# The means of the input's rows taken off x in place of off the weights, in a linear-attention and MLP-mixer kernel on one core

## The chip, the cores and the metric

The kernel runs on one core of one Trainium2 chip. The metric is the device time of one execution in microseconds; less is better. Times given for a kernel are medians of several executions; a profile is one further execution.

## The reference

The input x has 2048 rows of 512 columns. Each row is normalized, and two branches work on the result; the output is x plus the product of the first branch and a silu of the second. Cut to what matters:

```python
xn = _layernorm(x, axis=-1)
s = _A_ref(xn, A_wqkv, A_wo)           # linear attention, 32 heads of 16
g = _silu(_B_ref(xn, B_w1, B_w2, B_w3, B_w4))   # mixer block
return x + s * g

# _A_ref: q, k, v = xn @ wqkv
pq, pk = phi(q), phi(k)                # phi(t) = (t + 1 if t > 0 else exp(t)) + 1e-6
kv = einsum(pk, v); z = sum of pk over the rows
o = (pq @ kv) / (pq . z + 1e-6);  s = o @ wo

# _B_ref: h = gelu(_layernorm(xn) @ w1); its four quarters of 128 columns are shifted
# by +1, -1, +2 and -2 rows, then @ w2, x1 = xn + that;
# g = x1 + gelu(_layernorm(x1) @ w3) @ w4
```

The mean of a row has to be taken off before a product with wk, wq or w1. A product of the row less its mean with W is the product of the row with W less the mean times the sums of W's columns. So there are three ways: take the mean off x, subtract the column means from W once ("centring" W: then a row's mean drops out), or subtract mean times column sums from the product.

## The kernel before, in words

The rows are worked on in tiles of 128; four tiles (512 rows) are a block, and there are four blocks, b = 0 to 3. Products run in a split form: each operand is a rounded high part and a low rest, and a product is three passes, high x high, low x high, high x low (`products`). Pairs of tiles are multiplied by a scheme of seven quarter products in place of eight (`seven`, and for keys and queries `pair_kq`), which needs sums of operands (`forms_x`, `forms_q`, `forms_m`) and adds of results.

The stages, in order: load WK, WQ and the transposed input xt (`load_u`, which rounds it into u, high and low); the plain rows x for the means and variances (`load_rows`, `scale_x`); keys (`key`, `feature_k`) and queries (`query`), and the products of keys with rows (`gram`, tiles g), for block 0 singly, for block 1 half singly and half in pairs, for blocks 2 and 3 in pairs; the first mixer product with W1 (`mix1`, tiles h), with shifted rows and a halo of two columns at each edge of a block (`split_halo`); the second (`mix2`, tiles pbm, pem); the attention's matrix M from the grams, WV and WO; and then, block by block, the up products (tiles a, pa, pb, pe) and down products (acc) of the MLP, with the attention (`turn_q`, then for block 0 `attend`, tiles s, and for the others `forms_q` and `attend_pair`, tiles pas, pbs, pes) between them, and `gate` at the end.

How the means are handled before: WQ and W1 are centred by `Weights.center`: the four chunks are added on VectorE (for W1 by a load and three adding transfers, tile w1t), a full-precision product with ones gives the column sums in every row (tiles wqm, w1m), and four VectorE instructions subtract them from the weights. WK isn't centred: `sum_k` gets its column sums by eight products of its rounded chunks with ones (tile ksum), ScalarE makes wneg, their negative, and `feature_k` adds mean times wneg to a key's product. In `pair_kq`, ScalarE makes two tiles from wneg (ci, ck) for each pair, and two VectorE instructions add them. For blocks 2 and 3, `forms_x` takes two of its sums by loads and adding transfers (`by_dma`).

What sets the order: the program does not run in the order of the text. Every operation is recorded in a plan with an estimated duration (`Plan.add`), product by product; `deadlines` gives each product a nominal time and works back to a due time for everything that feeds it; `nudged` moves single due times by a table (SOONER); `emit` then takes, engine by engine, the operation that can start first by the plan's estimates, the one due soonest among equals, and writes it out. So each engine has a fixed order of its own and waits in it. Buffers are slots, 89 of tag "p", 4 accumulators and 4 product banks. Loads and stores are issued by SyncE (SP), adding transfers by GpSimd (POOL, `Plan.gather`). All TensorE instructions are recorded at line 146, ScalarE's at 168, most of VectorE's at 191, 196 and 201, loads at 207, stores at 212 and adding transfers at 225.

Of the kernel before, what the change touches and what calls it, by code (L numbers as in the profile page):

```python
# [85 lines left out]
class Plan:  # L86
# [54 lines left out]
    def mm(self, out, lhs, rhs, start, stop, slow=False, more=False, behind=None):  # L141

        nc = self.nc
        busy = 2 * (.0025 + .00083 * rhs.n) if slow else .0053 + .000444 * rhs.n
        self.add("PE", busy, busy + .17, [lhs, rhs], [behind or out],
                 lambda: nc.tensor.matmul(out.get(), lhs.get(), rhs.get(), start=start, stop=stop,  # L146
                                          skip_group_check=more))
# [81 lines left out]
    GAP = .06  # L229
    PATIENCE = 5.0  # L230
# [38 lines left out]
    def emit(self, first, lead, reserve, window, ahead, table=()):  # L269
# [20 lines left out]
        while left:  # L290
# [5 lines left out]
            for e, cands in avail.items():  # L296
                picks = []
                low = INF
                for op in cands:
# [11 lines left out]
                    for t in fresh:  # L311
# [7 lines left out]
                        s = max(s, q[need - 1][0] + self.GAP)  # L319
# [57 lines left out]
            for o in op.post:  # L377
# [5 lines left out]
                else:  # L383
                    r = op.end + self.GAP
# [11 lines left out]
def linear_attn_gated_by_mixer(  # L396
# [36 lines left out]
    counts = {"w": 2, "p": 89, "h": 6, "sm": 12, "ab": 2, "acc": 4, "mm": 4}  # L433
# [61 lines left out]
    onesr, bmask, few = fixed("onesr", P, F32R), fixed("bmask", P), fixed("few", 4)  # L495
# [3 lines left out]
    rs1, rs2, ns1, nm1, nm2, au, mr1 = (fixed(n, NT) for n in ("rs1", "rs2", "ns1", "nm1", "nm2", "au", "mr1"))  # L499
    arow = memory("arow", S + 2 * EDGE, 1)  # L500
# [18 lines left out]
    for o in (0, EDGE + S):  # L519
        pl.store(arow[:, o:o + EDGE], zacc[:1, :EDGE])  # L520
# [23 lines left out]
    class Weights:  # L544
# [25 lines left out]
        def center(self, by_dma=False):  # L570

            t, r = piece(self.name + "t"), self.raw
            if by_dma:
                pl.load(t, self.src[:, 0])
                for c in range(1, NC):
                    pl.gather(t, self.src[:, c])
            else:
                pl.tt(t, r[0], r[1], ALU.add)
                pl.tt(t, t, r[2], ALU.add)
                pl.tt(t, t, r[3], ALU.add)  # L580
            ps = bank(self.name + "m")
# [29 lines left out]
    def scale_x(lo, n):  # L611
# [7 lines left out]
        if lo >= QT:  # L619
# [11 lines left out]
    def spread_a(b):  # L631

        ps = pl.new("mm", f"ab{b}", F32, 512)[:QT, :P]
        pl.transpose(ps, au[:, b * QT:(b + 1) * QT], ident.all)
        t = pl.new("p", f"ar{b}", F32, PIECE)[:QT, :P]
        pl.act(t, ps, AF.Copy)
        row = arow[:, EDGE + b * BT:EDGE + (b + 1) * BT]
        pl.store(row.via(lambda ap: ap.rearrange("o (j p) -> (o j) p", p=P)), t)
# [11 lines left out]
    def load_u(b, parts):  # L650
# [3 lines left out]
        for q in range(parts):  # L654
            o = q * n
            for c in range(NC):
# [3 lines left out]
                pl.load(src, xt[b, c][:, o:o + n])  # L660
                hi, lo = (t[:, 2 + o:2 + o + n] for t in UT[b][c])
                if b == c == q == 0:
                    pl.ts(hi, src, 1.0, None, ALU.mult)
                    split(lo, src, hi)
                else:
                    rounded(hi, lo, src)

# [84 lines left out]
    def feature_k(i, ps):  # L752

        t, r = piece(f"kt{i}"), piece(f"kr{i}")
        pl.stt(t, wneg.all, mean(mv1, i), ps, ALU.mult, ALU.add)
# [9 lines left out]
    def key(i):  # L765
        ps = bank(f"k{i}")
        project(ps, i, WK, range(NC))
        feature_k(i, ps)
# [14 lines left out]
    def query(i):  # L783
# [3 lines left out]
        pl.act(z, ps, AF.Identity, scale=col(rs1, i), bias=one)  # L787
# [54 lines left out]
    def pair_kq(i):  # L842
# [32 lines left out]
        pl.stt(zk, pb, rk, ck, ALU.mult, ALU.add)  # L875
# [427 lines left out]
    wneg = fixed("wneg", 512)  # L1303
# [11 lines left out]
    load_u(0, 2)  # L1315
# [12 lines left out]
    sum_k(ksum, 0)  # L1328
    for c in range(1, NC):
        for i in range(2):  # L1330
            project(ks[i], i, WK, [c])
        sum_k(ksum, c)
    pl.act(wneg.all, ksum, AF.Copy, scale=-1.0)
# [6 lines left out]
    WQ.center()  # L1340
    WQ.split()
    gram(0)
    query(0)
    query(1)
    load_u(1, 1)
    for i in range(QT, 2 * QT):
        load_rows(i)
    gram(1)
# [6 lines left out]
    forms_x(1, 1)  # L1355
    early_s, early_f = EARLY
# [7 lines left out]
    for b in range(1, NQ):  # L1364
# [23 lines left out]
    pl.load(hal.all, halo.rearrange("p q c -> p (q c)"))  # L1388
    for b in range(NQ):
        scale_u(b)  # L1390
        spread_a(b)
# [15 lines left out]
    pool(.4, [], bmask.all, lambda: g.memset(bmask.all.get(), 0.5))  # L1407
    for base, s in ((0, 1), (DH - 1, -1)):
        v = bmask.all.via(lambda ap: ap.rearrange("p (h d) -> p h d", d=DH))
# [23 lines left out]
    for gg in range(NC):  # L1433
# [4 lines left out]
        pl.tt(kvt.cols(*cs), ps, bmask.all, ALU.mult)  # L1438
# [25 lines left out]
    for b in range(NQ):  # L1464
# [5 lines left out]
        for n, fs in enumerate(groups):  # L1470
# [11 lines left out]
            if b == 0 and 0 < n <= QT:  # L1482
                turn_q(n - 1)
            if b == 0 and 1 < n <= QT + 1:
                attend(n - 2)
            if b == 0 and n == QT:
                forms_m()
            pairs = []
            if b > 0:
                for k in range(2):  # L1490
                    if n == (2, 3)[k]:
                        for j in range(2):
                            turn_q(b * QT + 2 * k + j)
                        forms_q(b * QT + 2 * k)
                    if n == (4, 5)[k]:
                        pairs.append(b * QT + 2 * k)
# [102 lines left out]
```

## Time and profile before

| | before |
|---|---|
| median of 3 runs | 517.4 us (516.55 to 517.57) |
| profiled execution, its own time | 516.63 us |
| its span, first to last instruction | 514.9 us |
| granted TensorE clock | 0.999 |
| VectorE, ScalarE, GpSimd busy | 78%, 68%, 21% of the span |
| DMA | 105.24 MB, 204 GB/s in the mean |

The page names engines as PE (TensorE matmul), PEld (its weight loads), DVE (VectorE), ACT (ScalarE), POOL (GpSimd) and SP (SyncE); SPq and POOLq are the queues in which they issue transfers. Tile names stand as out<-in, with buffer numbers left out. The chain that ended last is followed back from the last instruction, at each step to what released it. Products are pipelined: a product's duration runs from its start to a modelled end and overlaps the next one, so what it costs is the step from its start to the start of the next.

### The profile page before, as it was taken

What the parts mean: (1) busy time and instruction counts of PE and PEld (TensorE: products, weight loads), DVE (VectorE), ACT (ScalarE), POOL (GpSimd) and SP (SyncE); (2) the same over time, 40 slices, a digit from 0 to 9 for tenths busy, and PEclk for the clock granted to TensorE, in tenths of its full rate; (3) what the DMA queues carried; (4) which work ended last, traced back from release to release, by engine and by line L of the source; (5) the groups of instructions that cost most, each with busy time, mean ns of one, the idle gap of its engine ahead of it and who ended that gap; (6) DMA issues with size and microseconds to landing.
All of it is one profiled execution on the core that took longest, in us unless ns stands there. A gap on an engine that the chain in (4) does not pass through costs nothing.

```text
span 514.9 us, 9112 instructions
## 1 busy us (share of the span) xinstructions
PE 508.0 (99%) x2987; PEld 440.4 (86%) x2987; DVE 402.0 (78%) x848; ACT 350.5 (68%) x759; POOL 109.4 (21%) x196
## 2 busy tenths in 40 slices
PE   8999999999999999999999999999999999999996
PEld 5778778877788897999899988899898998899985
DVE  4999998759989758999898649788576857497645
ACT  6797998977696678999986655467462555554621
POOL 3477163561100221232100022000230000410000
PEclk9999999999999999999999999999999999999999
DMA  7948858698642999899767589846499562897804
GB/s 230 281 112 225 238 178 212 169 225 231 137 153 71 229 287 273 246 282 305 266 220 240 197 199 235 239 152 178 113 192 308 162 209 91 176 293 219 274 3 120
DMA packets 77698, 105.24 MB, mean 204 GB/s; under 512 B 8228, under 2 KB 34356, under 8 KB 77652
## 3 DMA queue, kind: packets, MB, share of 16 engines
q1 hardware_dynamic: 67780, 87.63, 52.7%
q0 software_dynamic: 9872, 17.04, 20.0%
q8 instruction: 23, 0.38, 0.3%
q14 instruction: 23, 0.19, 0.1%
HBM read 69.64 MB, written 30.81 MB: 195 GB/s over the span
## 4 chain that ended last, share of the span: by engine, by line
PE 87%; ACT 4%; DMA 4%; DVE 2%; issue 2%; SPq 1%; POOL 0%; POOLq 0%; ACTq 0%; DVEq 0%
PE acc L146 21%; PE pb L146 11%; PE h L146 9%; PE g L146 7%; PE pe L146 5%; PE pbm L146 5%; PE pbx L146 4%; PE pbs L146 3%; PE q L146 3%; PE pa L146 2%; PE pem L146 2%; PE s L146 2%; PE pex L146 2%; PE pes L146 2%; PE a L146 2%
## 5 line engine op out<-in xcount | busy, mean ns | idle before, releaser
L225 POOL DMA_DIRECT2D xo<-x1d x12 | 10.6, 1034 | 151.5 <-ACT xo L168 151.0
L225 POOL DMA_DIRECT2D o<-xnd x16 | 13.9, 892 | 67.4 <-DMA w4d<-w_10l 29.8
L225 POOL DMA_DIRECT2D th<-in_x x14 | 12.1, 887 | 72.3 <-DVE th L201 62.5
L168 ACT ACTIVATE gf<-gf 128x512 f32<-128x512 f32 (+1 forms) x40 | 20.8, 522 | 0.8
L168 ACT ACTIVATE th<-xo 128x512 f32<-128x512 f32 (+1 forms) x16 | 9.7, 615 | 14.9 <-DVE xo L191 11.4
L168 ACT ACTIVATE p<-pe 128x256 f32<-128x256 f32 x20 | 7.6, 382 | 15.9 <-PE pe L146 15.6
L191 DVE TENSOR_TENSOR gf<-pa,p 128x256 f32<-128x256 f32 x20 | 8.3, 417 | 10.7 <-PE pa L146 7.3
L225 POOL DMA_DIRECT2D zacc<-ke x10 | 9.1, 911 | 29.8 <-DVE ke L201 14.2
L191 DVE TENSOR_TENSOR gf<-pb,p 128x256 f32<-128x256 f32 x20 | 8.4, 421 | 8.6 <-ACT p L168 4.6
L168 ACT ACTIVATE p<-pb 128x256 f32<-128x256 f32 x20 | 7.6, 380 | 9.0 <-PE pb L146 8.6
L191 DVE TENSOR_TENSOR f_10l<-gf,f_10h 96x512 fp32r<-96x512 f32 x4 | 2.7, 686 | 14.1 <-PE pb L146 13.9
L168 ACT ACTIVATE u<-pb 128x256 f32<-128x256 f32 x20 | 7.6, 382 | 8.8 <-PE pb L146 8.8
L191 DVE TENSOR_TENSOR ht<-h,abc 128x512 f32<-128x512 f32 x16 | 10.9, 689 | 2.7 <-PE h L146 2.6
L168 ACT ACTIVATE y<-o,nm,rs 128x512 f32<-128x512 f32 x16 | 11.8, 806 | 1.2 <-POOL nm L196 1.2
L196 POOL TENSOR_SCALAR w<-mv 128x4 f32<-128x4 f32 (+2 forms) x10 | 3.3, 329 | 43.3 <-DVE mv L196 42.9
L201 DVE SCALAR_TENSOR_TENSOR th<-th,so 128x512 f32<-128x512 f32 (+1 forms) x17 | 11.1, 659 | 1.5 <-ACT th L168 0.3
L168 ACT ACTIVATE xo<-acc 128x512 f32<-128x512 f32 x12 | 7.2, 598 | 7.3 <-PE acc L146 6.9
L168 ACT ACTIVATE ht<-ht 128x512 f32<-128x512 f32 x16 | 9.6, 623 | 3.4 <-DVE ht L191 3.4
L191 DVE TENSOR_TENSOR so<-so,xo 128x512 f32<-128x512 f32 (+1 forms) x16 | 10.7, 671 | 1.5 <-DMA xo<-x1d 1.3
L168 ACT ACTIVATE sq<-o,sx 128x512 f32<-128x512 f32 x16 | 11.4, 713 | 0.2 <-DVE sx L196 0.2
L201 DVE SCALAR_TENSOR_TENSOR qz<-pq,zb 128x512 f32<-128x512 f32 x16 | 10.9, 683 | 0.5 <-DMA pq<-pqd 0.5
L201 DVE SCALAR_TENSOR_TENSOR pq<-pq,rd 128x512 f32<-128x512 f32 x16 | 10.9, 688 | 0.3
(1717 smaller groups left out, 2277.1 us busy)
## 6 DMA issues: line engine op xcount, KB each, us to landing
w_s<-in_w SPq DMA_DIRECT2D x28, 256.0 KB, 5.3
x<-in_x SPq DMA_DIRECT2D x16, 256.0 KB, 4.6
xnd<-x SPq DMA_DIRECT2D x16, 256.0 KB, 3.8
pqd<-qr SPq DMA_DIRECT2D x16, 256.0 KB, 2.3
o<-xnd POOLq DMA_DIRECT2D x16, 256.0 KB, 6.7
x1d<-o SPq DMA_DIRECT2D x16, 256.0 KB, 4.7
pq<-pqd SPq DMA_DIRECT2D x16, 256.0 KB, 4.8
out<-th SPq DMA_DIRECT2D x15, 256.0 KB, 3.4
```

Of the source, the lines that this page charges most:

```text
L146: lambda: nc.tensor.matmul(out.get(), lhs.get(), rhs.get(), start=start, stop=stop, skip_group_check=more))
L168: nc.scalar.activation(out.get(), src.get(), func, scale=get(scale), **kw)
L191: self.vec(eng, out, [a, b], lambda: self.e(eng).tensor_tensor(out.get(), a.get(), b.get(), op=op), True)
L196: lambda: self.e(eng).tensor_scalar(out.get(), a.get(), get(s1), get(s2), **kw), False,
L201: lambda: self.nc.vector.scalar_tensor_tensor(out.get(), a.get(), get(s), b.get(), op0=op0, op1=op1),
L225: lambda: self.nc.gpsimd.dma_start(out.get(), get(src), accum_op=ALU.add), mb=mb)
```

## The change

Six things change.

- `load_u` for blocks 1 to 3, and once more for block 0 ahead of `mix1`, loads xt and then adds to it, by an adding transfer of POOL, a row of minus the means (nrow) that lies in memory and is broadcast over the partitions. `spread` makes that row: from the means and variances of the block's four tiles it puts two sets of four columns side by side (an), transposes them by one product (ab), copies it (ar) and stores it in two rows, arow (as before) and nrow. It now stands ahead of `load_u` of its block, and `load_rows` ahead of it. The halo has its means added too (`load_halo`).
- For block 0, xt is first used uncentred for its keys and queries: keys have mean times the column sums taken off as before, queries now likewise (qneg, cq).
- WQ and W1 aren't centred any more; keys of blocks 1 to 3 and the pairs have no term of means (ci, ck and their adds go).
- WK's column sums come from adding the four chunks on VectorE and one full-precision product, in place of eight products.
- Block 0's attention goes through `forms_q` and `attend_pair` as that of the other blocks. `forms_x` makes all its sums on VectorE.
- The plan: products are estimated a little shorter, an operation of another engine is taken to reach TensorE 0.16 us after its end in place of 0.06 (PE_GAP), there are 90 slots in place of 89, and a new SOONER table. The order of all engines is new.

```diff
-        busy = 2 * (.0025 + .00083 * rhs.n) if slow else .0053 + .000444 * rhs.n
+        busy = 2 * (.0025 + .00083 * rhs.n) if slow else .005 + .000443 * rhs.n
...
+    PE_GAP = .16
...
-                        s = max(s, q[need - 1][0] + self.GAP)
+                        s = max(s, q[need - 1][0] + (self.GAP if e != "PE" else self.PE_GAP))
...
-                    r = op.end + self.GAP
+                    r = op.end + (self.GAP if o.eng != "PE" else self.PE_GAP)
...
-        def center(self, by_dma=False):
...
-            if by_dma:
-                pl.load(t, self.src[:, 0])
-                for c in range(1, NC):
-                    pl.gather(t, self.src[:, c])
...
-            for c in range(NC):
-                pl.stt(r[c], ps, -1.0 / D, r[c], ALU.mult, ALU.add)
+        def sums(self, ps):
+            t, r = piece(self.name + "t"), self.raw
+            for c in range(1, NC):
+                pl.tt(t, t if c > 1 else r[0], r[c], ALU.add)
             pl.mm(ps, ones.all, t, True, True, slow=True)
...
-    def scale_u(b):
+    def spread(b):
+
+        u, m = (an[:, (2 * b + k) * QT:(2 * b + k + 1) * QT] for k in range(2))
         p = small(f"pu{b}", QT).all
         pl.ts(p, var(mv1, b * QT, b * QT + QT), 1.0 + EPS, EPS * EPS, ALU.mult, ALU.add, eng="POOL")
-        power(au[:, b * QT:b * QT + QT], p, QT)
+        pl.ts(m, means(mv1, b * QT, b * QT + QT), -1.0, None, ALU.mult, eng="POOL")
+        power(u, p, QT)
+        ps = pl.new("mm", f"ab{b}", F32, 512)[:2 * QT, :P]
+        pl.transpose(ps, an[:, 2 * b * QT:2 * (b + 1) * QT], ident.all)
+        t = pl.new("p", f"ar{b}", F32, PIECE)[:2 * QT, :P]
+        pl.act(t, ps, AF.Copy)
+        for k, row in enumerate((arow, nrow)):
+            dst = row[:, EDGE + b * BT:EDGE + (b + 1) * BT]
+            pl.store(dst.via(lambda ap: ap.rearrange("o (j p) -> (o j) p", p=P)),
+                     t.via(lambda ap, k=k: ap[k * QT:(k + 1) * QT]))
...
                 pl.load(src, xt[b, c][:, o:o + n])
+                if centred:
+                    pl.gather(src, nrow[:, EDGE + b * BT + o:EDGE + b * BT + o + n].via(
+                        lambda ap: ap.to_broadcast([P, n])))
...
-    def sum_k(ps, c):
-
-        for n, p in enumerate(WK.chunk(c)):
-            pl.mm(ps, onesr.all, p, c == n == 0, c == NC - 1 and n == 1)
...
-        pl.act(z, ps, AF.Identity, scale=col(rs1, i), bias=one)
+        if i < QT:
+            cq = piece(f"cq{i}")
+            pl.act(cq, qneg, AF.Identity, scale=col(mr1, i), bias=one)
+            pl.stt(z, ps, col(rs1, i), cq, ALU.mult, ALU.add)
+        else:
+            pl.act(z, ps, AF.Identity, scale=col(rs1, i), bias=one)
...
-        ci, ck = piece(f"ci{i}"), piece(f"ck{i}")
-        for t, n in ((ci, i), (ck, k)):
-            pl.act(t, wneg.all, AF.Identity, scale=col(mr1, n), bias=one)
         go(pb, "a11", "b11")
-        pl.stt(p1, pb, ri, ci, ALU.mult, ALU.add)
+        copy(p1, pb, ri)
...
-            load_u(b + 1, 1)
             for j in range(QT):
                 load_rows(t0 + QT + j)
+            spread(b + 1)
+            load_u(b + 1, 1)
             scale_x(t0 + QT, QT)
-            forms_x(b + 1, by_dma=True)
+            forms_x(b + 1)
...
-            W1.center(by_dma=True)
...
+    load_u(0, 1)
+    load_halo()
...
-            if b == 0 and 0 < n <= QT:
-                turn_q(n - 1)
-            if b == 0 and 1 < n <= QT + 1:
-                attend(n - 2)
-            if b == 0 and n == QT:
+            pairs = []
+            if b == 0 and n == 3:
                 forms_m()
-            pairs = []
-            if b > 0:
-                for k in range(2):
...
+            for k in range(2):
+                if n == (2, 3)[k] if b == 0 else n == (2, 3)[k]:
+                    for j in range(2):
+                        turn_q(b * QT + 2 * k + j)
+                    forms_q(b * QT + 2 * k)
+                if n == (4, 5)[k] if b == 0 else n == (4, 5)[k]:
+                    pairs.append(b * QT + 2 * k)
```

More of the change, by code (lines that the diff above doesn't have):

```diff
@@ L519, in linear_attn_gated_by_mixer @@
     for o in (0, EDGE + S):
-        pl.store(arow[:, o:o + EDGE], zacc[:1, :EDGE])
+        for row in (arow, nrow):
+            pl.store(row[:, o:o + EDGE], zacc[:1, :EDGE])
     def mean(mv, i):
@@ L666, in load_u, with load_halo @@
                     rounded(hi, lo, src)
+    def load_halo():
+        hm = small("hm", NQ * W)
+        pl.load(hal.all, halo.rearrange("p q c -> p (q c)"))
+        for o, k in ((-2, 0), (BT, 2)):
+            dst = hm.cut([(0, NQ * W)], 2 * NQ, lambda ap, k=k: ap.rearrange("p (b w) -> p b w", w=W)[:, :, k:k + 2])
+            src = nrow.cut([(0, S + 2 * EDGE)], S, lambda ap, o=o: ap[:, EDGE + o:EDGE + o + S].rearrange(
+                "o (b n) -> o b n", n=BT)[:, :, :2].to_broadcast([P, NQ, 2]))
+            pl.fetch(dst, src)
+        v = hal.all.via(lambda ap: ap.rearrange("p (b c w) -> p b c w", c=NC, w=W))
+        m = hm.all.via(lambda ap: ap.rearrange("p (b w) -> p b w", w=W)[:, :, None, :].to_broadcast([P, NQ, NC, W]))
+        pl.tt(v, v, m, ALU.add, eng="POOL")
     def split_halo(b):
@@ L754, in feature_k @@
         t, r = piece(f"kt{i}"), piece(f"kr{i}")
-        pl.stt(t, wneg.all, mean(mv1, i), ps, ALU.mult, ALU.add)
+        pl.stt(t, wneg, mean(mv1, i), ps, ALU.mult, ALU.add)
         pl.act(r, t, AF.Relu, scale=col(rs1, i))
@@ L874, in pair_kq @@
         go(pb, "a22", "t4", False)
[L875 removed]
+        copy(zk, pb, rk)
         phi_q(k, qk)
@@ L1331, in linear_attn_gated_by_mixer @@
             project(ks[i], i, WK, [c])
-        sum_k(ksum, c)
-    pl.act(wneg.all, ksum, AF.Copy, scale=-1.0)
+    WK.sums(ksum)
+    pl.act(wneg, ksum, AF.Copy, scale=-1.0)
     for i in range(2):
@@ L1339, in linear_attn_gated_by_mixer @@
     WQ = Weights("wq", wqkv[0])
-    WQ.center()
     WQ.split()
+    qp, qneg = bank("qsum"), piece("qneg")
+    WQ.sums(qp)
+    pl.act(qneg, qp, AF.Copy, scale=-1.0)
     gram(0)
```

59 lines of the change are left out of this document (23 added, 36 removed), and 50 rows, old and new, of the table SOONER.

## The prediction

> **What bounds the kernel now.** I read the head of the page first, then the chain, then the waits of TensorE, then the first 30 us of its timeline.
>
> ```profile
> span 514.9 us, 9112 instructions
> PE 508.0 (99%) x2987; PEld 440.4 (86%) x2987; DVE 402.0 (78%) x848; ACT 350.5 (68%) x759; POOL 109.4 (21%) x196
> ...
> PE 87%; ACT 4%; DMA 4%; DVE 2%; issue 2%; SPq 1%; POOL 0%; POOLq 0%; ACTq 0%; DVEq 0%
> ```
>
> TensorE is busy for 508.0 of 514.9 us and holds 87% of the chain. The view of waits, for PE alone, says how little it waits for others (total, times, longest):
>
> ```profile
> PE warm L146 <- POOL ones L506: 1.0, 1, 1.0
> PE ksum L146 <- ACT wk_1h L168: 0.3, 1, 0.3
> PE pb L146 <- DVE gf L191: 0.3, 1, 0.3
> PE pbx L146 <- DVE p1x L201: 0.3, 1, 0.3
> PE k L146 <- ACT u_1h L168: 0.3, 1, 0.3
> ```
>
> That is 2.2 us in all. So the time is the sum of the products' issue steps: taking products away shortens it directly, and a new wait on PE lengthens it directly. The steps come from the chain (start, us, what) and, below it, the timeline of PE (start, duration):
>
> ```profile
> 150.66 11.13 PE h L146 x48
> 277.10 2.48 PE s L146 x21
> 508.00 2.38 PE accx L146 x20
> ```
>
> ```profile
> 13.26 0.39 PE L146 MATMUL ksum<-wk_3h,onesr 128*128 128x512 f32 x1
> 13.49 0.39 PE L146 MATMUL ksum<-wk_3l,onesr 128*128 128x512 f32 x1
> 19.32 1.02 PE L146 MATMUL wqm<-wqt,ones 128*128 128x512 f32 x2
> 20.19 0.97 PE L146 MATMUL g<-k0h,x0h 128*128 128x512 f32 x3
> 23.80 0.40 PE L146 MATMUL q<-wq_0h,u_0l 128*128 128x512 f32 x1
> 24.34 0.50 PE L146 MATMUL q<-wq_0h,u_0h 128*128 128x512 f32 x1
> ...
> 26.87 0.39 PE L146 MATMUL q<-wq_2h,u_2h 128*128 128x512 f32 x1
> 27.26 0.50 PE L146 MATMUL q<-wq_2l,u_2h 128*128 128x512 f32 x1
> ```
>
> A row's duration (0.39) is longer than its step, since products overlap. A step of 512 columns is 11.13/48 = 0.232 us, of 256 columns 2.48/21 = 0.118 us, and a full-fp32 product of 512 columns, which runs in two passes, holds PE from 19.32 to 20.19, 0.87 us. PE's last product ends at 508.00 + 2.38 = 510.4; what PE isn't busy besides its waits is the tail behind it, 4.5 us.
>
> **The change part by part.** The base is the profiled execution: 516.63 us, of which 514.9 is span. It lies 0.8 us under the median of the runs (517.4).
>
> *WK's sums.* Eight ksum products go (8 x 0.232 = 1.86) and one fp32 product comes (0.87): **-0.99**. The DVE adds that feed it (three of 512 columns) run beside PE. Bounds: three of the eight stand ahead of the two starting waits for wk_1h and u_1h; if the data come no earlier, their 0.70 only lengthens those waits and -0.29 is left. On the other side x0's load is moved from the sixth place of SP's queue to the tenth, so xt0_1 lands after 896 KB in place of 1,280 KB, and both waits (0.6) may go: -1.59. I keep the middle.
>
> *W1 no longer centred.*
>
> The views of the tiles w1m and wqm (durations in ns, least, median, most; first and last start):
>
> ```profile
> L146 PE MATMUL w1m<-w1t,ones x2: 590/590/591, 125.5 to 125.9; 128*128 128x512 f32 x2
> L201 DVE SCALAR_TENSOR_TENSOR wq_s<-wqm,wq_s x4: 681/683/685, 21.0 to 23.6; 128x512 f32<-128x512 f32 x4
> ```
>
> The same two passes as wqm: **-0.87**. With it go four DVE instructions, a load and three POOL gathers, none on the path.
>
> *WQ no longer centred.* The product stays (qsum for wqm). What goes is the chain from it through DVE's four wq_s instructions (from 21.0 to 23.6 + 0.68 in the row above) to the q products. q's step from 23.80 to 24.34 is 0.54 and that from 26.87 to 27.26 0.39, in place of 0.232 each: 0.3 and 0.16 of waiting. I take **-0.4**, bounds -0.7 and 0. Late next are four added DVE instructions that put the means back in q of block 0, behind PE.
>
> *Block 0's attention.* The order of instructions shows 96 products of 256 columns before and 84 after, 12 x 0.118 = **-1.42**. What it costs is DVE work: 16 instructions of 256 columns and two more of 512, net.
>
> Two of the page's groups (xcount | busy, mean ns), and three stretches (length, PE, PEld, DVE, ACT, POOL, clock, DMA, GB/s):
>
> ```profile
> L191 DVE TENSOR_TENSOR gf<-pa,p 128x256 f32<-128x256 f32 x20 | 8.3, 417 | 10.7 <-PE pa L146 7.3
> ...
> L191 DVE TENSOR_TENSOR ht<-h,abc 128x512 f32<-128x512 f32 x16 | 10.9, 689 | 2.7 <-PE h L146 2.6
> ```
>
> ```profile
> 240.00:260.00 20.00, 19.98 (x137) 17.97 (x136) 18.13 (x52) 19.57 (x50) 5.37 (x8) 1.00 0.75 236
> 260.00:280.00 20.00, 20.00 (x137) 18.26 (x137) 19.29 (x40) 14.59 (x32) 0.00 (x0) 1.00 0.84 270
> 280.00:300.00 20.00, 20.00 (x120) 17.66 (x119) 13.41 (x23) 11.96 (x25) 0.00 (x0) 1.00 0.56 186
> ```
>
> DVE is busy 50.8 of 60 us, so 9.2 are free; added are 16 x 0.417 + 2 x 0.689 = 8.1. ACT, 46.1 busy, has 13.9 free and gains 3. It just fits, and the new order spreads single acc products between those of the attention, which PE can do meanwhile: 0. If the cover isn't there, see below.
>
> *The means off x.* Block 1's xt now waits for the means of its rows: DVE's row statistics, two small POOL results, a transposition on PE (ab), an ACT copy, a store to memory, a load that adds them in (a POOL gather), and only then the rounding. PE is in order, so both the ab product and the first k product of block 1 can stand and hold all behind them. By the order of instructions 39 products lie between the two: 39 x 0.232 = 9.0 us of cover. Queued behind it: on ACT behind ar, exp of q and k; on SP behind the store (itself behind two x loads), stores of q and x that nobody needs soon; on POOL behind the four gathers, block 2's statistics, which have time. The links, from the timelines and the chain, then from the tile ab, then from the DMA issues (us to landing last):
>
> ```profile
> 36.01 2.46 DVE L593 BATCH_NORM_STATS2 st<-x 128x6 f32<-128x512 f32 x4
> 42.42 0.94 POOL L225 DMA_DIRECT2D zacc<-kr  x1
> 44.27 1.11 POOL L609 TENSOR_TENSOR au<-pu,nhalf 128x4 f32<-128x4 f32 x1
> 45.51 1.28 POOL L225 DMA_DIRECT2D xf<-in_xt  x1
> 34.61 0.62 ACT L168 ACTIVATE u_1h<-xt 128x512 fp32r<-128x512 f32 x1
> 43.76 1.61 PE k L146 x7
> ```
>
> ```profile
> L151 PE MATMUL ab<-ident,au x4: 270/270/272, 133.6 to 134.9; 128*4 128x128 f32 x4
> L168 ACT ACTIVATE ar<-ab x4: 249/250/266, 134.0 to 135.2; 4x128 f32<-4x128 f32 x4
> ```
>
> ```profile
> w4d<-w_0h SPq DMA_DIRECT2D x1, 256.0 KB, 2.2
> x1d<-o SPq DMA_DIRECT2D x16, 256.0 KB, 4.7
> w1t<-in_w POOLq DMA_DIRECT2D x3, 256.0 KB, 4.7
> o<-xnd POOLq DMA_DIRECT2D x16, 256.0 KB, 6.7
> abc<-arow SPq DMA_DIRECT2D x4, 258.0 KB, 4.6
> ```
>
> Product 0.27, copy 0.25, store 2.2 to 4.7, gather 4.7 to 6.7, rounding 0.62: 8.0 to 12.5 us against 9.0, so a wait of 0 to 3.5 at the k products. Above it, the statistics: ab stands 9.0 us ahead of the k of 43.76 (less the 1.4 saved by then), near 33.3. The statistics ran at 36.01, but in the new order some ten DVE instructions of 0.6 that stood ahead now follow, and xt's loads come behind the x rows: they run at 28 to 30, with 2.46, the aggregation and 1.11 + 0.5 on POOL to 32.5 to 34.5: 0 to 1.2 at ab. Together 0 to 4.7. The nearest rows (a gather from memory into SBUF, 4.7, and a broadcast row of the same kind on SP, 4.6, no slower than plain loads) speak for the low end: **+1.0**, half at each.
>
> The Trainium skill ("DMA: Bandwidth & Descriptors", Anatomy of one DMA — SWDGE (gpsimd) path) fits a gather's time as 2.0 us plus bytes/436e3, an estimate of 2.6 us here; by it the k wait would be nothing and the sum 0.5 lower. The rows above, 4.7 to 6.7, do not agree, and stand.
>
> Blocks 2 and 3 have the same chain under 65 and 57 products (15.1 and 13.2 us) against 12.5: 0. The reloaded xt of block 0 waits for nothing late. Queues: POOL issues 16 gathers more and 7 fewer, SP 7 issues more.
>
> ```profile
> q0 software_dynamic: 9872, 17.04, 20.0%
> ```
>
> 65 gathers take 20.0% of 514.9, 1.6 us of all engines each; nine more are 14 us, mostly between 30 and 125 us, where no PE wait on a DMA is on the list above: 0.
>
> *Tail and order.* The last 38 products are the same ones in the same order as in the row of accx: 0. The new order elsewhere may gain or lose within what PE waits now: 0, bounds -0.6 and +1.
>
> Sum: -0.99 - 0.87 - 0.4 - 1.42 + 1.0 = **-2.7**, 513.9 against the profiled execution. Half of its distance to the median added, **514.3 us**.
>
> **The rivals.** *The chain of the means is late (slower).* Place: ab and the k products of block 1. Beyond the 4.7 above, the four gathers follow each other; each chunk feeds nine products, 2.1 us, and a gather that shares the engines with x8 to x11 may land 0.6 later than the last one's products end, three times: 6.5 in place of 1.0, 514.3 + 5.5 = **519.8**. For it: order on PE leaves no other work ahead of it. Against: gathers of 1.6 us fit in 2.1. It turns the sign from a wait of about 5.
>
> *The change doesn't do what it says at the start.* The start is paced by loads, ksum stood in front of waits, and wkt's DVE adds are late for the one product: -0.29 in place of -0.99, and nothing from q: 1.1 less, **515.4**. For it: the two waits of 0.3; against: at 13.3 us the step of ksum is 0.23, so PE was full there.
>
> *DVE becomes the bound in block 0.* Of its 9.2 free us 6.6 lie in 280 to 300, behind part of the added 8.1; if 2.5 don't fit ahead and PE's spare acc products run out, **516.8**.
>
> *POOL's issues are held by DVE.* A gather's issue took 0.94 in one row and 1.28 in another while DVE was busy. If each of the added ones is held 0.4 at block 1, only the first delays k, +0.4: **514.7**. The Trainium skill (the same page, SWDGE vs HWDGE vs iDMA) says that DVE in its two-port mode locks POOL out of the memory where it writes a gather's descriptors; no row here separates that.
>
> **How the numbers follow.** Forecast 0.57 (its own range 512.6 to 515.8), late chain 0.14, start 0.12, DVE 0.10, POOL 0.07. A measurement of this kernel can tell about 0.2%, 1.0 us, from no change. Faster takes the forecast, the start and POOL: 0.76; the late chain is slower, 0.13, with 0.01 of it and DVE's 0.10 within: 0.11. The range leaves out most of the late chain and the forecast's lower edge: 512.4 to 517.3.
>
> **What would show it.** PE instructions about 20 fewer in the profile, PE busy about 3.3 less; no ksum row but one of two passes; q's steps even; waits of PE on ar, an or u_ of block 1 of about 1 us. A wait of over 5 there, DVE at 20 of 20 us between 240 and 290 with PE waiting for q or s tiles, or an unchanged first g at 20.2 would each make the prediction wrong at its step.

## The result and the profile after

The changed kernel takes **509.14 us** (median of 4 executions, 508.64 to 509.31), the kernel before in the same measurement 516.97 (516.22 to 517.57): 0.985 of it, interval 0.983 to 0.987. That is 7.8 us faster; the forecast was 514.3 and its range ended at 512.4. The sign was right, and the gain was two and a half times the 3.1 us forecast (514.3 against 517.4).

The head of the page of the changed kernel, and the engines' shares of its chain (its profiled execution took 508.64 us):

```profile
span 506.9 us, 9090 instructions
...
PE 500.1 (99%) x2967; PEld 436.9 (86%) x2967; DVE 403.6 (80%) x865; ACT 354.1 (70%) x772; POOL 118.0 (23%) x210
...
PE 90%; ACT 4%; DMA 3%; DVE 1%; SPq 1%; issue 1%; DVEq 0%
```

PE has 20 instructions fewer, as forecast, but its busy time fell by 7.9 us, not by 3.3. PE's waits (total, times, longest), which answer to the 2.2 us of before:

```profile
PE warm L146 <- POOL ones L508: 1.0, 1, 1.0
PE k L146 <- ACT u_0h L168: 0.5, 1, 0.5
PE k L146 <- DVE u_0l L191: 0.2, 1, 0.2
PE pbm L146 <- DVE o L191: 0.2, 1, 0.2
PE g L146 <- ACT k0h L168: 0.2, 1, 0.2
```

They sum to 2.1 us, the same as before. So the gain above the forecast lies neither in fewer products nor in listed waits. It lies in PE's *busy* time, which needs another measure.

**A measure for what the page doesn't show.** Products overlap, so a product that starts late still touches the one ahead of it and no idle time appears. I took the start of every product and the start of the next (all 2,987 and 2,967 rows) and subtracted the least step of its kind: 0.232 us for 512 columns, 0.118 for 256, and 0.432, 0.220 and 0.112 for a pass of full fp32 with 512, 256 and 128 columns. The sum of the least steps is called the *work* here, the rest the *holds*. Both in us:

| | work | holds | 0 to 21 us | 21 to 240 | 240 to 300 | from 300 |
|---|---|---|---|---|---|---|
| before | 498.37 | 10.79 | 3.67 | 3.59 | 0.83 | 2.70 |
| after | 495.09 | 6.00 | 3.84 | 1.45 | 0.11 | 0.60 |

The work fell by 3.28, which is the prediction's three terms of products to the hundredth (0.99 + 0.87 + 1.42). Since the work is counted with the same least steps that the prediction used, this confirms its counts of products; whether the time follows them is tested further down. The other 4.8 are holds, gone everywhere but in the first 21 us; 2.1 of them stood behind 300 us, where both kernels compute the same (the changed kernel, being ahead, has done 40 of before's 1,396 products there by then).

How a hold looks. The rows are the first product of a group in the up stage of the MLP, which waits for a factor of DVE or ACT (xcount | busy, mean ns of one | listed idle), first of before, then of after:

```profile
L146 PE MATMUL pb<-yt43h,w_b 128*128 128x256 f32 x20 | 4.8, 302 | 0.3 <-DVE gf L191 0.3
L146 PE MATMUL pb<-yt41h,w_b 128*128 128x256 f32 x20 | 4.6, 293 | 0.0
L146 PE MATMUL pb<-yt40h,w_b 128*128 128x256 f32 x20 | 4.5, 286 | 0.0
```

```profile
L146 PE MATMUL pb<-yt40h,w_b 128*128 128x256 f32 x20 | 4.5, 280 | 0.0
L146 PE MATMUL pb<-yt41h,w_b 128*128 128x256 f32 x20 | 4.5, 285 | 0.0
L146 PE MATMUL pb<-yt43h,w_b 128*128 128x256 f32 x20 | 4.5, 285 | 0.0
```

The same product, with no idle time listed, lasts 293 ns on average in the one and 285 in the other. A mean over its fellows' 280 is the trace of a wait. One such wait in before's timeline of PE:

```profile
450.48 0.27 PE L146 MATMUL pa<-yb213h,w_al 128*128 128x256 f32 x1
451.06 0.38 PE L146 MATMUL pb<-yt43h,w_b 128*128 128x256 f32 x1 [0.30 <-DVE gf L191]
451.28 0.28 PE L146 MATMUL pb<-yt43l,w_b 128*128 128x256 f32 x1
```

From 450.48 to 451.06 is 0.58 in place of 0.118, and the next step is 0.22 in place of 0.118, because the first product behind a gap lasts 0.38. The gap costs 0.56 us; the view of waits shows 0.30 of it, and for a gap shorter than the overlap it shows nothing.

**The links that the prediction priced**, in the timelines of PE, ACT, SP and POOL (start, duration), and the DMA issues:

```profile
12.61 1.02 PE L146 MATMUL ksum<-wkt,ones 128*128 128x512 f32 x2
...
18.66 0.97 PE L146 MATMUL g<-k0h,x0h 128*128 128x512 f32 x3 [0.16 <-ACT k0h L168]
19.47 1.02 PE L146 MATMUL qsum<-wqt,ones 128*128 128x512 f32 x2
```

```profile
32.40 0.27 PE L151 MATMUL ab<-ident,an 128*8 128x128 f32 x1
```

```profile
32.71 0.27 ACT L168 ACTIVATE ar<-ab 8x128 f32<-8x128 f32 x1
...
40.77 0.62 ACT L168 ACTIVATE u_0h<-xt 128x512 fp32r<-128x512 f32 x1
```

```profile
33.00 0.27 SPq L212 DMA_DIRECT2D nrow<-ar  x1
```

```profile
35.04 3.57 POOL L225 DMA_DIRECT2D xt<-nrow  x4
```

```profile
41.42 0.39 PE L146 MATMUL q<-wq_3l,u_3h 128*128 128x512 f32 x1
41.65 0.39 PE L146 MATMUL k<-wk_0h,u_0h 128*128 128x512 f32 x1
```

```profile
xt<-nrow POOLq DMA_DIRECT2D x16, 256.0 KB, 7.2
```

The sums of WK are one row of two passes, and the first g starts at 18.66 in place of 20.19. Of these 1.53 us, 0.87 are the order's: WQ's product, which stood ahead of the first g (wqm, 19.32), now stands behind it (qsum). So 0.66 of WK's 0.99 has arrived there, and the rest went into holds; those of the first 21 us rose by 0.17.

The chain of the means takes 9.25 us from ab (32.40) to the first k of block 1 (41.65), u_0h is done at 41.39, and k follows the product ahead of it by 0.23: no wait, with 0.26 us to spare. The first gather, issued at 35.04, landed at 39.04 by the trace's semaphores, so u_0h stood another 1.7 us in ACT's order before it began.

### The profile page after: what moved, and what is told of

The parts are those of the page before. It is cut to its first block, busy times and chain, and to the rows that moved or that the text cites. A ratio compares the mean times of both kernels' runs of the same rounds, so it can differ in the third digit from the quotient of the medians.

```text
span 506.9 us, 9090 instructions
## 1 busy us (share of the span) xinstructions
PE 500.1 (99%) x2967; PEld 436.9 (86%) x2967; DVE 403.6 (80%) x865; ACT 354.1 (70%) x772; POOL 118.0 (23%) x210
## 4 chain that ended last, share of the span: by engine, by line
PE 90%; ACT 4%; DMA 3%; DVE 1%; SPq 1%; issue 1%; DVEq 0%
PE acc L146 23%; PE pb L146 11%; PE g L146 9%; PE h L146 7%; PE pe L146 6%; PE pbx L146 6%; PE pbs L146 4%; PE q L146 3%; PE pbm L146 3%; PE pa L146 3%; PE pex L146 3%; PE pes L146 2%; PE a L146 2%; PE pem L146 2%; DMA w4d<-w_2h 2%; PE pax L146 1%
## 5 line engine op out<-in xcount | busy, mean ns | idle before, releaser
L225 POOL DMA_DIRECT2D zacc<-ke x12 | 12.4, 1036 | 31.4 <-DVE u_2l L191 10.1
L168 ACT ACTIVATE th<-xo 128x512 f32<-128x512 f32 (+1 forms) x16 | 9.7, 615 | 11.2 <-DVE xo L191 10.8
L191 DVE TENSOR_TENSOR gf<-pa,p 128x256 f32<-128x256 f32 x20 | 8.4, 418 | 11.1 <-PE pa L146 10.8
L225 POOL DMA_DIRECT2D xt<-nrow x16 | 14.3, 1224 | 9.2 <-ACT xs_3h L168 6.8
L191 DVE TENSOR_TENSOR gf<-u,pe 128x256 f32<-128x256 f32 x20 | 8.3, 414 | 8.4 <-PE pe L146 7.7
L168 ACT ACTIVATE sq<-o 128x512 f32<-128x512 f32 x16 | 10.0, 628 | 2.1 <-DMA o<-xnd 2.1
L191 DVE TENSOR_TENSOR so<-pas,p1s 128x256 f32<-128x256 f32 x8 | 3.4, 423 | 9.6 <-PE pas L146 6.2
```

Source lines behind the costliest of these rows:

```text
L168: nc.scalar.activation(out.get(), src.get(), func, scale=get(scale), **kw)
L191: self.vec(eng, out, [a, b], lambda: self.e(eng).tensor_tensor(out.get(), a.get(), b.get(), op=op), True)
L225: lambda: self.nc.gpsimd.dma_start(out.get(), get(src), accum_op=ALU.add), mb=mb)
```

## The experiments

Three theories of the 4.8 us: **A**, the plan's new estimates (PE_GAP 0.16 in place of 0.06, and the products' durations); **B**, the order that the new SOONER table makes; **C**, the changed work, which relieves other engines. Times are medians; "before" is the kernel before in the same measurement (516.25 to 517.09).

**Estimates and table changed over.** e1 is the kernel before with the new estimates, e2 the changed kernel with the old ones:

```diff
-        busy = 2 * (.0025 + .00083 * rhs.n) if slow else .0053 + .000444 * rhs.n
+        busy = 2 * (.0025 + .00083 * rhs.n) if slow else .005 + .000443 * rhs.n
+    PE_GAP = .16
```

> The kernel before with one thing of the change: the plan's estimates (PE_GAP .16 and the two numbers of a product's duration); its table of due times and all its work stay. The profiles say that TensorE's steps above their least (0.232 and 0.118 us) sum to 10.8 us before and 6.0 after. Theory A, the estimates: products are placed when their inputs have really arrived, so most of those 4.8 us go: 512.5 to 513.5 us. Theory B, the table: found for another plan it fits worse here, 516 to 519. Theory C, the changed work relieves the other engines: 517 within 0.5.

> The changed kernel with the plan's estimates of before (PE_GAP .06 and the old durations), its own table and work kept. Theory A: the small holds come back, 509.1 + 3 to 4.8 = 512 to 514. Theory B: the table is off too, 510 to 513, which doesn't tell it from A alone; with e1 it does. Theory C: 509.1 within 0.7.

e3 is the kernel before without a table, e5 the changed kernel without one:

```diff
-    SOONER = (
...
+    SOONER = ()
```

> The kernel before with an empty table of due times, estimates and work as before. Theory B: the table is worth 3 to 6 us, 520 to 523. Theories A and C: 517 to 519.

> The changed kernel with an empty table, its estimates kept. Theory B: the 4.8 us that the fixed work does not explain are the new table's, so 513 to 515. Theories A and C: 509 to 511.

| | time | ratio to before | holds | 0 to 21 | 21 to 240 | 240 to 300 | from 300 |
|---|---|---|---|---|---|---|---|
| e1 | 516.09 | 0.9992 [0.9981, 1.0004] | 9.49 | 4.42 | 2.76 | 0.94 | 1.38 |
| e2 | 518.5 | 1.0042 [1.0027, 1.0057] | 15.47 | 3.96 | 4.28 | 4.48 | 2.75 |
| e3 | 521.3 | 1.0098 [1.0075, 1.0121] | 15.74 | 3.95 | 5.08 | 1.95 | 4.75 |
| e5 | 518.0 | 1.0039 [1.002, 1.0057] | 16.30 | 3.33 | 5.41 | 6.35 | 1.20 |

The new estimates alone bring the kernel before nothing that its interval can tell from no change (0.4 us). A table is worth 4.8 us to it (521.3 to 516.46) and 8.9 to the changed kernel (518.0 to 509.14); each was made for its own work and its own estimates. e2 and e5 came out above every range expected of them. Without tables the changed kernel is 3.3 us faster (e5 against e3), as much as its fewer products save, but that is luck: e5 holds 4.4 us more in block 0's attention and 3.6 less from 300 us on, and the two plan with different estimates. So C looks unlikely and B likely, but A isn't nothing. Sorted by length from 21 us on, the holds of 0.02 to 0.1 us number 70 in before (3.6 us), 65 in e3 and 85 in e2, which plan with 0.06; with 0.16 they number 19 in after (1.2 us), 23 in e1, 28 in e5. In every later run, all with 0.16, they are 12 to 35. e2's groups show it, the changed kernel's own products with the old estimates:

```profile
L146 PE MATMUL pb<-yt40h,w_b 128*128 128x256 f32 x20 | 5.0, 305 | 0.1
L146 PE MATMUL pb<-yt41h,w_b 128*128 128x256 f32 x20 | 4.8, 298 | 0.0
```

Planned 0.06 us behind its factor, a product stands on PE's queue before the factor is there, and each pays about a tenth. e1 gets rid of those 2.4 us but holds 1.1 more elsewhere, 0.75 of it in the first 21 us; that its table, found for the old estimates, is the cause is likely but not shown. How the gap and the durations share the effect is open: they weren't tried apart.

e5 also shows what the table hides. Its waits of PE:

```profile
PE k L146 <- ACT u_0h L168: 1.6, 1, 1.6
...
PE pbs L146 <- DVE m_t2l L191: 0.9, 1, 0.9
PE pbs L146 <- DVE so L191: 0.6, 1, 0.6
```

PE now waits at both places that two of the prediction's rivals name. In block 0's attention it waits for late tiles of DVE, as that rival says. At the first k of block 1 the cause is another than the rival's: the first gather landed at 41.35 us, before PE was free at 42.54, but ACT took squares of x (sq) first and came to u_0h at 43.45. So it is ACT's order that costs the 1.6 us, not the gathers.

**Half a table.** e8 keeps the 182 entries ahead of block 0's up stage and ends with the pair 2292, 27; e9 keeps the 117 behind it (an entry is an operation's number and how many quarters of a us it is due sooner):

```diff
     SOONER = (
-        35, -10, 38, -73, 50, 78, 52, 42, 65, -23, 68, 6, 70, 16, 89, 28, 104, -6, 106, 21, 107, -47, 108, -10,
...
+        2295, -20, 2296, -26, 2310, -19, 2381, 4, 2387, -23, 2396, -30, 2401, -28, 2403, -15, 2418,
...
```

> The changed kernel with only the 182 entries of its table that stand before block 0's up stage (operations under 2295); the 117 later ones are left out. What is computed is the same. Without any table the kernel took 518.0 us, with all of it 509.1. Theory B1 (each stretch owes its even pace to the entries of that stretch): the start to 225 us keeps its pace, and the holds of block 0's attention (6.35 us between 240 and 300 us without the table, against 0.11 with it) and of the rest (1.20 against 0.60) come back: 509.1 + 6.8 = 516. Rival B2 (the early entries decide, since loads and buffers that come on time early stay on time): 509 to 511. Rival B3 (the tables only work as a whole): 518 or more.

> The changed kernel with only the 117 later entries (operations from 2295 on). B1: the holds ahead of 225 us come back (8.8 us without the table against 5.3 with it), block 0's attention stays even: 509.1 + 3.5 = 512.6. B2 (early entries decide): 516 to 518. B3 (only as a whole): 518 or more, since the later entries were chosen for another state.

e8 513.22 (0.9943 [0.992, 0.9965]), e9 514.41 (0.9963 [0.9951, 0.9975]). None of the three fits alone. e9 has the early holds of e5 back in full (5.46 between 21 and 240 us, against 5.41), as B1 says; but in e8 only 2.91 of the 6.35 us in block 0's attention return, and in e9 2.38 stay although its entries are there. Each half is worth about half, and what an early part leaves behind decides with the later one.

**Two parts undone, without a table.** e10 takes block 0's attention back to eight products; e11 takes WK's sums back to eight one-pass products.

```diff
             pairs = []
-            if b == 0 and n == 3:
+            if b == 0 and 0 < n <= QT:
+                turn_q(n - 1)
+            if b == 0 and 1 < n <= QT + 1:
+                attend(n - 2)
+            if b == 0 and n == QT:
                 forms_m()
```

```diff
-    WK.sums(ksum)
+    sum_k(ksum, c)        # in the loops over the chunks, as before
```

> The changed kernel without any table (518.0 us) and with block 0's attention as in the kernel before: eight products of each size, 96 in place of 84, without the 18 DVE instructions. If the rival of the prediction holds in that order (DVE is the bound of the stage, 6.35 us of holds between 240 and 300 us), the holds fall to some 2 us as in the kernel before without its table (1.95) and the 12 products cost 1.4: 518.0 - 4.4 + 1.4 = 515, and PE waits for m, so and q0s1 tiles are gone. If the holds there are only a matter of order, 12 products more cost 1.4: 519.4.

> The changed kernel without any table (518.0 us) and with WK's sums as before: eight products of one pass each in place of one of two passes. By the prediction's sum +1.0: 519.0, the first g about 1 us later. If the start is paced by its loads, +0.3: 518.3. If an order of its own decides (theory B), the rest moves by up to 2 us either way and the first 20 us alone show it.

e10 515.58 (0.9983 [0.9973, 0.9993]), as expected: holds of 1.13 between 240 and 300 us in place of 6.35. In this order seven products cost 2.4 us more than eight. e11 525.35 (1.0158 [1.0114, 1.0201]), a miss by 6 us: the products' work rose by the forecast 0.99, and the first 21 us held 3.9; but the order moved, u_0h of block 1 came behind a full ACT, and PE's timeline and the stretches (length, PE, PEld, DVE, ACT, POOL, clock, DMA, GB/s) show this:

```profile
48.01 0.80 PE L146 MATMUL k<-wk_0h,u_0h 128*128 128x512 f32 x1 [4.37 <-ACT u_0h L168]
...
49.03 0.63 PE L146 MATMUL q<-wq_0h,u_0h 128*128 128x512 f32 x1
```

```profile
48.00:50.00 2.00, 1.99 (x5) 1.62 (x6) 0.95 (x2) 2.00 (x4) 0.89 (x3) 0.50 1.11 269
50.00:52.00 2.00, 2.00 (x6) 1.55 (x5) 1.47 (x3) 2.00 (x4) 0.94 (x1) 0.50 1.05 404
52.00:54.00 2.00, 2.00 (x7) 1.57 (x6) 1.93 (x7) 1.56 (x3) 0.00 (x0) 0.57 1.09 362
54.00:56.00 2.00, 2.00 (x10) 1.65 (x9) 1.54 (x4) 0.00 (x0) 0.00 (x0) 1.00 1.08 318
```

That is the place of the prediction's late chain, again without its cause (the first gather landed at 40.88, PE was free at 43.64, and ACT came to u_0h at 47.34), and with a price that it did not know. Behind the wait of 4.4 us the granted clock is 0.50, and 13 products run at steps of 0.43 in place of 0.23 until 53.7 us: 2.5 us more. (The Trainium skill, "TensorE: Matmul & The Clock Gate", Part 1: The HAM clock gate, says that an idle window of about 3.4 us halves the clock. This row agrees, as does e5's wait of 1.6 us at the same place, behind which the clock stays 1.00; e12 below does not, where it falls to 0.50 behind a wait of 1.6 us.) The profiled execution, 526.43 us, is the slowest of four that begin at 521.43. In it the clock falls a second time, in block 0's attention (0.50 from 286 to 290 us), where e11 holds 1.1 us more than e5.

**Does before's work have such an order too?** In these runs the estimates are the new ones and only the table is edited, as above. The tables come from a random local search over due times. The first search took the planner's own timetable as its measure (tables of some 4,000 entries):

> The kernel before, with the new estimates and a table that was newly found for it, by a random local search over the planner's own due times (as many tries as the next run's). Its work is that of the kernel before, 2,987 products of 498.4 us by their least steps. If the even pace of the changed kernel comes from a better order alone (theory B, the order belongs to the search and not to the change), the holds of before, 10.8 us, fall towards the 6.0 of the changed kernel: 509.1 + 3.3 to 4 = 512.5 to 513. If the changed work itself makes the even pace possible (theory C again), the holds stay over 9: 516 or more.

> The changed kernel with its own table carried on by the same search, the same number of tries. Theory B: what is left of the holds (6.0 us, of it 3.8 in the first 21 us, which wait for loads and for POOL's ones) can fall by 1 at most: 508 to 509.1, faster than both kernels by up to 0.2%. If the search only fits the planner's estimates and not the chip, 509 to 511.

e12 519.1 (1.0036 [1.0018, 1.0055]), e13 523.82 (1.0137 [1.0091, 1.0184]): both slower, with holds of 13.2 and 20.1, and e13 above both of its ranges. I took it that the orders were tight against transfers that land later than the planner takes; no run isolates that. The second search therefore wanted orders that stay good when transfers and instructions are late at random:

> The work of the kernel before (2,987 products), the new estimates, and a table of 121 entries found by the same kind of search, but for orders that stay good when each transfer lands later by some random 0.5 us and each other instruction takes a little longer. The search without that slack broke (519.1 us, its holds at loads and late factors). Theory B (the order alone makes the even pace; any of the two kernels' work can have it): holds of 6 to 8 in place of 10.8, 512.5 to 514.5, faster than before by 0.5% or more. Theory C (the changed work is needed for it): 516 or more.

> The work of the changed kernel, with a table of 150 entries found by the same search with slack, starting from its own table, of which 6 entries are left. Theory B, with the fixed work 3.3 us under that of the kernel before: 509 to 511, and 3 to 4 us under the run of before's work with the same search. If the table of the changed kernel is a singular find: 512 or more.

> The changed kernel with block 0's attention in eight products again (12 products of 256 columns more, 1.42 us; 18 DVE instructions fewer), with a table of 126 entries found by the same search with slack, started from no table. If the prediction's term holds in a good order (seven products save 1.4 and their DVE work hides), it takes 1.4 more than the run with seven: 510.5 to 512.5. If the DVE work of the seven costs what it costs without a table (2.4 us net, 518.0 against 515.6), it is no slower than the run with seven.

e14 516.7 (1.0006 [0.9992, 1.002]), e15 510.6 (0.9898 [0.9875, 0.9921]), e16 515.54 (0.998 [0.996, 0.9999]). By the letter C wins here, e15 lies where B expects it, and e16 meets neither of its two expectations. But e14 and e16 have 5.2 and 7.2 us of holds in the first 21 us, against 3.7 and 3.8. There their products still step at 0.43 us up to 9 and 13 us, while before's step at 0.23 from 5.9 us on; whether the order or chance did that isn't shown. And e14 has one hold of 2.15 us that explains itself. Its DVE group, DVE's timeline and PE's:

```profile
L191 DVE TENSOR_TENSOR so<-so,xo 128x512 f32<-128x512 f32 (+1 forms) x16 | 10.6, 668 | 6.3 <-DMA xo<-x1d 6.2
```

```profile
450.15 0.69 DVE L191 TENSOR_TENSOR so<-so,xo 128x512 f32<-128x512 f32 x1 [2.47 <-DMA xo<-x1d]
450.75 0.42 DVE L191 TENSOR_TENSOR gf<-pb,p 128x256 f32<-128x256 f32 x1
```

```profile
451.23 0.38 PE L146 MATMUL pb<-yt43h,w_b 128*128 128x256 f32 x1 [1.99 <-DVE gf L191]
```

The gate's product so, which nobody needs soon, waits for a POOL gather; the factor gf stands behind it on DVE, and PE behind gf. In before the same group waits 1.3 us for these gathers (first row), and in the changed kernel for none (second row):

```profile
L191 DVE TENSOR_TENSOR so<-so,xo 128x512 f32<-128x512 f32 (+1 forms) x16 | 10.7, 671 | 1.5 <-DMA xo<-x1d 1.3
L191 DVE TENSOR_TENSOR so<-so,xo 128x512 f32<-128x512 f32 (+1 forms) x16 | 10.6, 668 | 0.1
```

The hold of 0.56 us in before, shown above, ends the same way: in the chain (start, us, what) it stands behind such a gather, from which so, two factors and PE follow.

```profile
440.46 8.23 DMA xo<-x1d
451.06 0.97 PE pb L146 x6
```

The third search kept the entries of the first 220 operations, the first 20 us, from the table of before or of the changed kernel, and took gathers 1 to 3 us later than the planner does (tables of about 200 entries; e17 starts from e14's, e18 from before's, e19 from the changed kernel's; e20 has the edit of e10):

> The work of the kernel before, the new estimates, and a third search: the order of the first 20 us is left as it was (the second search made it 1.5 us worse), and orders must stay good when POOL's gathers land 1 to 3 us later than the planner thinks (in the second search one such gather held PE for 2.15 us). It starts from the second search's table. Theory B: the holds fall to 6 to 8 (10.8 before), 512 to 514. Theory C (the changed work is needed): 516 or more.

> The same, with the table of the kernel before as its start. Theory B: 512 to 514; theory C: 516 or more. If the two differ by over 2 us, a search of this kind says little of either.

> The work of the changed kernel with the third search, started from its own table: 508 to 510, within 1 us of the changed kernel, and by theory B 3 to 4 us under the better one of before's work.

> The changed kernel with eight products in block 0's attention, the third search: by the prediction's term 1.4 us more than the run with seven of the same search, 510 to 511.5; its first 20 us keep the order of the changed kernel, so that the start (7.2 us of holds in the second search, against 3.8) doesn't mask the term. If seven products cost DVE time that no order hides: 509 or less.

| | time | ratio to before | work | holds | 0 to 21 | 21 to 240 | 240 to 300 | from 300 |
|---|---|---|---|---|---|---|---|---|
| e17, before's work | 512.19 | 0.9918 [0.99, 0.9937] | 498.37 | 6.14 | 4.39 | 1.32 | 0.01 | 0.41 |
| e18, before's work | 513.91 | 0.9931 [0.9906, 0.9956] | 498.37 | 8.11 | 3.53 | 4.04 | -0.03 | 0.57 |
| e19, changed work | 508.89 | 0.9851 [0.9835, 0.9867] | 495.09 | 5.72 | 4.06 | 1.36 | 0.04 | 0.26 |
| e20, eight products | 510.81 | 0.9886 [0.987, 0.9903] | 496.51 | 5.89 | 4.07 | 1.58 | 0.05 | 0.21 |

e17 has the kernel before's 2,987 products and the changed kernel's holds. Its page, its waits of PE, and the groups that were 302 and 286 ns:

```profile
span 510.2 us, 9096 instructions
...
PE 503.4 (99%) x2987; PEld 440.9 (86%) x2987; DVE 402.8 (79%) x848; ACT 348.8 (68%) x759; POOL 110.5 (22%) x196
```

```profile
PE g L146 <- ACT k0h L168: 1.2, 1, 1.2
PE warm L146 <- POOL ones L507: 1.0, 1, 1.0
```

```profile
L146 PE MATMUL pb<-yt43h,w_b 128*128 128x256 f32 x20 | 4.4, 280 | 0.0
L146 PE MATMUL pb<-yt40h,w_b 128*128 128x256 f32 x20 | 4.4, 281 | 0.0
```

C falls: with the new estimates and an order of its own, before's work takes 512.19 us, 4.1 less than before, as B expects. e17 has both, so it does not tell A from B; the estimates alone (e1) gained nothing clear. e19 is then faster than e17 by 3.30, the work's 3.28; that they agree so closely is luck, as each of the two times is known to about 1 us. e20 is 1.9 slower than e19: 1.42 of work for its 12 products, 0.17 of holds, and 0.3 that these sums don't explain. e19 is as fast as the changed kernel (508.70 to 509.07 against 508.64 to 509.31), not faster beyond doubt; no version was clearly better. e18, 1.7 us above e17, gives an idea of how far such a search scatters, though its own five executions already lie between 511.77 and 514.21.

## Why the prediction was wrong

**Right, in mechanism and size.** PE bounds the kernel. The three terms of products, 0.99 + 0.87 + 1.42, came out as 3.28 of work; e17 against e19 gives 3.30 and e20 against e19 tests the largest of them by itself. The q chain: the holds between 21 and 45 us fell by 0.65, against 0.4 forecast with bounds 0.7 and 0; but e17, which still centres WQ, has lost 0.49 of before's 0.85 there too, so the size is right and the cause not shown. Tail: from the start of PE's last product to the end 4.8 us before (510.08 to 514.9) and 4.9 after (502.02 to 506.9), unchanged.

**Block 0's attention.** "It just fits, 0" holds in the order that runs, by these stretches of the changed kernel, PE full and DVE at 55.98 of 60 us:

```profile
240.00:260.00 20.00, 20.00 (x127) 18.01 (x126) 19.72 (x47) 17.87 (x44) 2.18 (x4) 1.00 0.88 295
260.00:280.00 20.00, 20.00 (x142) 18.71 (x142) 19.78 (x43) 15.85 (x37) 0.00 (x0) 1.00 0.86 237
280.00:300.00 20.00, 20.00 (x127) 17.86 (x126) 16.48 (x31) 12.22 (x26) 3.55 (x4) 1.00 0.53 159
```

The prediction named DVE at 20 of 20 with PE waiting as the sign of the rival. DVE came to 19.8 and PE did not wait; in e5, at the same DVE load (55.9 of 60), PE did. Of the 8.1 us that the prediction added to DVE, 5.2 show in these 60 us, and ACT, to which it added 3, stands at 45.9 in place of 46.1. A free share of an engine says that an order can exist, not that it does.

**The means off x, +1.0: mis-sized, 0 measured.** The chain took 9.25 us, inside its 8.0 to 12.5, and the cover of 39 products was enough. At ab nothing waited either, as the row statistics ran at 25.5 us and not at 28 to 30. The links came out at 2.0 us from store to gather and 4.0 for the gather, both below what was taken, and 1.7 in ACT's order, a link that the sum did not have. The margin is 0.26 us. In e5 and e11 PE waited 1.6 and 4.4 us at that place (with the clock 6.9), through that link and not through late gathers, which were the rival's reason. So the rival named the right place with the wrong cause, and with no price for the clock.

**The step that failed** is the last one of the sum: "The new order elsewhere may gain or lose within what PE waits now: 0, bounds -0.6 and +1." The forecast fell short by 5.3 us (2.7 against 8.0 between the profiled executions). 1.0 of it is the term of the means; 4.4 belong to this step, the 4.8 us by which the holds fell less the 0.4 forecast for q (the tail grew by 0.1). The bound was taken from the view of waits, 2.2 us in all, but that view leaves out the holds under the overlap of two products, and before had 10.8 us of holds. Of the 8.0 of them from 21 us on (sums of those over 0.02 us), holds up to 0.1 us fell from 3.6 to 1.2 and longer ones from 4.4 to 2.0. The first go with the new estimates, by the counts of all 19 traces; the second mostly with the table, as e1 with before's table still has 4.7 of them, and the late gather of before and e14 is one kind of them shown to the end. What share the new gap has in the first, apart from the products' durations, stays open.

The data for a better bound were there. The prediction priced each product at its least step, rightly, but never set the sum of all least steps, 498.4 us, beside the 509 us between PE's first and last product. The 10.8 between them, less the 3.3 to 4 at the start that no order of these runs removed, was what a new order could give.

## What to carry to other kernels

Where one in-order engine is busy for 99% of the time, sum its steps against the least step of each kind before bounding what a new order can give: busy time contains waits, and a first product whose mean lasts longer than its fellows' is where to look. A change that comes with a new order must be compared with the old work in an equally good order, or the order's gain is booked to the change; here only 3.3 of the 7.8 us belong to the changed work. An instruction that waits for a transfer belongs behind whatever the bound engine needs next, however little it costs itself.

## What the runs showed of the hardware

- Behind a wait of 4.4 us of PE its granted clock was 0.50 for 5.7 us more (e11, 48.0 to 53.7), at a price of 2.5 us. A wait of 1.6 us left it at 1.00 in e5, but behind one of 1.6 us in e12 (ending at 308.9) it fell to 0.50 for some 3.4 of these 4 us (columns as above):

```profile
310.00:314.00 4.00, 4.00 (x20) 3.86 (x19) 2.73 (x8) 1.49 (x5) 0.86 (x1) 0.57 1.09 285
```

- It also fell without so long a wait. In e5, block 0's attention, no listed wait of PE was over 0.9 us, yet PE was busy for only 2.67 of 4 us and then ran at 0.61 (the same columns). So no single long wait explains these rows:

```profile
278.00:282.00 4.00, 2.67 (x14) 1.90 (x13) 3.98 (x8) 2.77 (x6) 0.00 (x0) 0.96 0.76 215
282.00:286.00 4.00, 4.00 (x19) 3.61 (x19) 3.33 (x9) 1.85 (x5) 0.00 (x0) 0.61 0.40 110
```

- The first 256-column product behind a gap lasts 0.38 us in place of 0.28 and delays its follower by 0.1; short holds of 0.1 and less, most of which no view lists as a wait, cost the kernel before 3.6 us.
- A POOL gather of 256 KB that adds a broadcast row from memory landed in 6.6 to 8.1 us (medians of the kernels that have it), against 4.7 to 6.7 for the gathers that the prediction took. The medians hide a queue: block 1's four in the changed kernel, issued together from 35.04 us on, landed 4.0 us after issue for the first and 8.9 for the last, 2.0 to 2.4 us apart.
